# Attention with four heads a tile and exp columns as matmul weights, in a fused attention and feed-forward kernel

## The chip, the core and the metric

One core of a Trainium2 chip runs the whole program. The metric is device microseconds (us) of one execution, median of several runs. The kernel before took 488.79 us (three runs, 488.09 to 491.07). Runs more than 1.5% above the fastest of the same kernel count as slow and are not in the ratios.

Engines: TensorE (PE; its weight loads are PEld), VectorE (DVE), ScalarE (ACT), GpSimd (POOL) and SyncE (SP, which here only issues transfers).

## The reference

```python
# q, k, v: (8 batches, 12 heads, 448, 64) float32; tau = 0.1
q_n = q / (norm(q) + 1e-6);  k_n = k / (norm(k) + 1e-6)
scores = q_n @ k_n.T / tau
attn = softmax(scores);  x = (attn @ v)          # heads side by side: (3584, 768)
h = x @ w_in                                     # 768 -> 2048
g = h * sigmoid(1.702 * h)
out = g @ w_out                                  # 2048 -> 768
```

The kernel computes in float16 with float32 sums.

## The kernel before

It is written as a list of operations with durations, dependences and buffers. A small planner simulates them and emits each engine's instructions in the resulting order; engines then run in that order, as the changed kernel's trace shows: the last copy into the first scores' qkT ended at 16.26 us, but TensorE stood 0.50 us before the next transposes in its list, did them from 16.34 us, and began the scores at 17.09 us. So a duration in the list changes the order only.

Attention works on a pair of heads. The 448 positions lie as 4 chunks of 112 on partitions. Scores are keys by queries, so that exp gives the values product its operand without a transpose (code shortened):

```python
def scores(x, c):                       # one chunk of 112 keys, both heads: two matmuls on 64 rows
    for j in range(2):
        nc.tensor.matmul(out=sp[:, j, :S], lhsT=qkT[64*j:64*(j+1), 1, c*P:(c+1)*P],
                         rhs=qkT[64*j:64*(j+1), 0, :], start=True, stop=True)

def attend(x, j):                       # batches 2 to 7: v as weights, 448 exp columns streamed
    for c in range(C):
        nc.tensor.matmul(out=ps, lhsT=vts[x % NV][:, c, j], rhs=exps[x, c][:, j], ...)

def attend_h(x, h):                     # batches 0 and 1: 112 exp columns as weights, 65 of v streamed
    for i in range(2):
        for j in range(2):
            for c in range(C):
                at = (c % 2) * SH + i * P
                nc.tensor.matmul(out=ps[:P, o:o+D+1], lhsT=exps[x, h, c // 2][:, j, at:at+P],
                                 rhs=vts[x % NV][:, c, j, 63*j:63*j+D+1], ...)
```

`attend` gives the output transposed, with the softmax denominators in a row. To divide, the kernel sends the denominators through DRAM and back, spread over partitions (six transfers for three pairs). From batch 1 on, q and k are turned (transposed) by DMA; in batch 0 by TensorE. PSUM is shared out in buffers of 512 float32 columns: four for scores, three for the expert products and `attend_h` ("mm"), one for `attend`.

## Time and profile before

| | busy us of 485.7 | share |
|---|---|---|
| TensorE | 452.7 | 93% |
| ACT | 304.8 | 63% |
| DVE | 278.3 | 57% |
| POOL | 147.2 | 30% |
| DMA engines, 120 to 420 us | | 50% |

Read such a table with the stretches of time beside it: of TensorE's 33 us of idle time 23 lie in the first 80 us, and 5.4 between 120 and 420 us, where its own work is what counts.

### The profile page before, as it was taken

The page shows a single profiled execution, that of the slowest core. Times are in us where ns is not written, and L with a number is a line of the kernel's source. Part 1 is how long each engine was busy: PE and PEld are TensorE (multiplying, and loading weights), DVE is VectorE, ACT ScalarE, POOL GpSimd, SP SyncE. Part 2 cuts the span into 40 slices and gives each one's busy share as a digit, 9 for nine tenths or more (in the row PEclk, how much of TensorE's full clock was granted, in tenths as well). Part 3 has the DMA queues.
Part 4 walks back from the last instruction along what each step waited for, and adds up shares of the span by engine and source line. Part 5 has one row for each costly group of instructions (what it writes and reads, how often), then busy time and mean ns, then how long its engine had stood idle before and what let it go on. Part 6 is the DMA issues. An engine that isn't in the chain of part 4 may idle for free.

```text
span 485.7 us, 8249 instructions
## 1 busy us (share of the span) xinstructions
PE 452.7 (93%) x3008; PEld 253.5 (52%) x3008; DVE 278.3 (57%) x657; ACT 304.8 (63%) x479; POOL 147.2 (30%) x201
## 2 busy tenths in 40 slices
PE   0599995999998999999989999999999999999996
PEld 0477885864443554445434554445444554455563
DVE  7834784687689845866397645874264315532500
ACT  4755672899977676775776676774576546523411
POOL 1454675156751731406060421506000000000000
PEclk9999998999999999999999999999999999999999
DMA  9999299979977655647653556534320222022022
GB/s 207 230 236 252 44 198 146 270 195 268 248 205 166 154 151 167 138 97 193 143 140 101 144 140 170 133 94 122 86 47 3 61 67 61 2 62 66 0 57 75
DMA packets 87000, 64.83 MB, mean 133 GB/s; under 512 B 45800, under 2 KB 80432, under 8 KB 86960
## 3 DMA queue, kind: packets, MB, share of 16 engines
q1 hardware_dynamic: 83072, 57.79, 48.6%
q0 software_dynamic: 3648, 6.29, 7.1%
q8 instruction: 23, 0.38, 0.3%
q10 hardware_dynamic: 240, 0.23, 0.1%
q14 instruction: 17, 0.14, 0.1%
HBM read 49.81 MB, written 11.14 MB: 125 GB/s over the span
## 4 chain that ended last, share of the span: by engine, by line
PE 72%; DMA 12%; DVE 6%; SPq 4%; issue 2%; ACT 2%; POOL 2%; ACTq 0%; POOLq 0%; DVEq 0%
PE mm L546 28%; PE mm L491 18%; PE avp L356 8%; PE sp L337 6%; PE mm L402 4%; PE sp L385 3%; PE mm L521 3%; DMA qkT<-qks 3%; DMA k<-in_k_dram 2%; DMA q<-in_q_dram 2%; SPq L221 2%; DMA dnm<-den 2%; DMA v<-in_v_dram 2%; DVE xT L480 2%; POOL qks L291 1%
## 5 line engine op out<-in xcount | busy, mean ns | idle before, releaser
L348 ACT ACTIVATE expT<-sp 112x896 f16<-112x896 f32 x192 | 167.3, 918 | 60.1 <-PE sp L337 41.9
L546 PE MATMUL mm<-w_out,gT 128*128 128x384 f16 x896 | 154.6, 326 | 0.4 <-ACT ost L557 0.4
L491 PE MATMUL mm<-xT,w_in 128*128 128x448 f16 x672 | 134.6, 353 | 4.0 <-DVE gT L508 3.9
L546 PEld LDWEIGHTS <-gT 128*128 128x128 f16 x896 | 83.9, 98 | 65.6 <-issue 13.7
L491 PEld LDWEIGHTS <-w_in 128*128 128x128 f16 x672 | 63.1, 98 | 70.7 <-issue 16.0
L508 DVE SCALAR_TENSOR_TENSOR gT<-th,mm 128x448 f16<-128x448 f16 x112 | 67.7, 617 | 53.8 <-ACT th L501 53.5
L501 ACT ACTIVATE th<-mm 128x448 f16<-128x448 f32 x128 | 69.4, 546 | 44.2 <-PE mm L491 33.3
L240 DVE TENSOR_REDUCE n<-sq 112x8 f32<-112x512 f32 x96 | 63.7, 678 | 31.2 <-ACT sq L234 29.4
L303 POOL CAST vt<-v 112x256 f16<-112x256 f32 x84 | 33.9, 418 | 151.4 <-PE avp L356 116.9
L373 DVE TENSOR_SCALAR av<-avp 65x448 f16<-65x448 f32 x72 | 44.4, 616 | 48.9 <-PE avp L356 48.6
L356 PE MATMUL avp<-expT,vt 112*128 112x448 f16 x288 | 66.4, 352 | 1.4 <-DVE av L373 1.4
L291 POOL TENSOR_TENSOR qks<-k,y 112x512 f16<-112x512 f32 x48 | 50.8, 1058 | 49.7 <-DVE y L281 31.1
L557 ACT ACTIVATE ost<-mm 128x384 f32<-128x384 f32 x56 | 27.6, 492 | 45.3 <-PE mm L546 43.6
L291 POOL TENSOR_TENSOR qks<-q,y 112x512 f16<-112x512 f32 x47 | 49.8, 1061 | 0.0
L337 PE MATMUL sp<-qkT 64*112 64x448 f16 x288 | 43.0, 372 | 0.0
L480 DVE TENSOR_TENSOR xT<-av,rcb 64x448 f16<-64x448 f16 x72 | 36.7, 510 | 10.6 <-DMA rcb<-rcp 9.6
L356 PEld LDWEIGHTS <-vt 112*128 112x128 f16 x288 | 27.9, 97 | 26.4 <-issue 2.0
L234 ACT ACTIVATE sq<-k 112x512 f32<-112x512 f32 x42 | 26.5, 634 | 16.1 <-DMA k<-in_k_dram 14.6
L402 PE MATMUL mm<-vt,expT 112*112 112x65 f16 x384 | 30.9, 242 | 3.0 <-ACT expT L348 2.7
L402 PEld LDWEIGHTS <-expT 112*112 112x112 f16 x384 | 28.7, 161 | 6.3 <-ACT expT L348 3.7
L234 ACT ACTIVATE sq<-q 112x512 f32<-112x512 f32 x42 | 26.4, 633 | 7.7 <-DVE n L240 5.1
L385 PE MATMUL sp<-qkT 64*112 64x224 f16 x192 | 20.6, 325 | 8.1 <-DMA qkT<-qks 4.9
(39 smaller groups left out, 193.5 us busy)
## 6 DMA issues: line engine op xcount, KB each, us to landing
k<-in_k_dram SPq DMA_DIRECT2D x48, 224.0 KB, 3.7
v<-in_v_dram SPq DMA_DIRECT2D x48, 224.0 KB, 4.3
q<-in_q_dram SPq DMA_DIRECT2D x47, 224.0 KB, 4.3
rcb<-rcp SPq DMA_DIRECT2D x24, 168.0 KB, 3.5
w_in<-in_moe_w_in_dram POOLq DMA_DIRECT2D x2, 1536.0 KB, 16.8
w_out<-in_moe_w_out_dram POOLq DMA_DIRECT2D x2, 1536.0 KB, 14.6
out_dram<-ost SPq DMA_DIRECT2D x7, 336.0 KB
out_dram<-ost SPq DMA_DIRECT2D x8, 288.0 KB
```

The source lines that it names most:

```text
L234: return nc.scalar.activation(out=sqs[x, ti], in_=src, func=AF.Square)
L240: nc.vector.tensor_reduce(out=n2s[grp][:, x - grp[0], ti], in_=sqs.pop((x, ti)), axis=AX.X, op=ALU.add,)
L291: return eng.tensor_tensor(out=qkss[x][:, ti].rearrange("p c j d -> p j c d"), in0=src, in1=rss[x][:, ti, :, :, None].to_broadcast((P, 2, ...
L337: nc.tensor.matmul(out=sp[:, j, :S], lhsT=qkT[64 * j : 64 * (j + 1), 1, c * P : (c + 1) * P], rhs=qkT[64 * j : 64 * (j + 1), 0, :], start= ...
L348: nc.scalar.activation(out=e, in_=sps.pop(key)[:, :, :S], func=AF.Exp, scale=inv_tau, **kw)
L356: nc.tensor.matmul(out=ps, lhsT=vts[x % NV][:, c, j], rhs=exps[x, c][:, j], start=(c == 0), stop=(c == C - 1),)
L402: nc.tensor.matmul(out=ps[:P, o : o + D + 1], lhsT=exps[x, h, c // 2][:, j, at : at + P], rhs=vts[x % NV][:, c, j, 63 * j : 63 * j + D + 1 ...
L480: nc.vector.tensor_tensor(out=xT[r], in0=av[r, j], in1=rcbs[x // GRP][r, x % GRP], op=ALU.mult)
L491: nc.tensor.matmul(out=ps[:, :S], lhsT=w_in_sb[:, kk, 128 * m : 128 * (m + 1)], rhs=xTs[b, kk], start=(kk == 0), stop=(kk == KT1 - 1),)
L501: nc.scalar.activation(out=ths[key], in_=mms[key][:, :S], func=AF.Tanh, scale=0.851)
L508: nc.vector.scalar_tensor_tensor(out=gts[b // 2][:, m, (b % 2) * S : (b % 2 + 1) * S], in0=ths.pop((b, m)), scalar=1.0, in1=mms.pop((b, m) ...
L546: nc.tensor.matmul(out=mms[b2, t, n][:, :NW], lhsT=gts[b2][:, kk, 128 * t : 128 * (t + 1)], rhs=w_out_sb[:, kk, NW * n : NW * (n + 1)], st ...
```

## The change

The intent: the same mathematics with fewer and fuller instructions. q and k come four heads at a time on 128 partitions (7 column blocks of 64 positions), so keys fall in three chunks of 128 and a half chunk. The half chunks of two heads make one full-height product. The values product uses exp columns as weights in every batch, 128 of them, so the output has positions on partitions, the denominators lie beside it, and the round trip through DRAM goes.

```diff
-    C = S // P
+    C = S // 64
-    ps_s = psum("ps_s", 2);  ps_a = psum("ps_a", 1);  ps_m = psum("ps_m", 3)
+    ps_s = psum("ps_s", 2);  ps_m = psum("ps_m", 4)
 ...
+    def scores(y, *chunks):            # two chunks of 128 keys in a row
+        for g, n in chunks:
+            sp = sps[y, g, n] = ps_s.tile([128, 2, 512], FP32, name="sp")
+            score(sp, y, g, n, 0, S, 0)
+    def scores_l(y, h=None):           # half chunks of two heads: one product on 128 rows
+        for g in range(2):
+            nc.tensor.matmul(out=sp[:, g, :S], lhsT=kLs[y % NE][:, g], rhs=qkTs[y][:, g, 0], ...)
 ...
+    def attend(x, h, short=False):     # 14 matmuls: 2 of 130 columns, 12 of 65
+        for i in range(2):
+            a, m = P * (2 * h + i), P if short and i else 128
+            nc.tensor.matmul(out=o, lhsT=e[:, (C-1)*S + a : (C-1)*S + a + m], rhs=vt[:, 3] ...)
+            for n in range(3):
+                for j in range(2):
+                    at = (2 * n + j) * S + a
+                    nc.tensor.matmul(out=o[:, (D+1)*j : (D+1)*(j+1)], lhsT=e[:, at : at + m], rhs=vt[:, n, j], ...)
 ...
-    den_out, den_in, den_rcp, rcp_out, rcp_in, normalise   # the round trip through DRAM
+    dma_turn_x                                              # the output turned by DMA (batches 2 to 7)
+    TURNED = 2 * ND                     # batches 0 and 1: q, k and the output turned on TensorE
```

(Lines are joined and arguments left out. Cut: loads of v in four pieces, norms by Ln and Exp on ACT in batch 0, casts of v on POOL, w_in in eight pieces, new durations.)

## The prediction

> **What bounds the kernel now.** I read the page's busy table and slices first, then busy time by stretch, then the instructions in order of time, then the costliest groups, and the waits last.
>
> ```profile
> PE 452.7 (93%) x3008; PEld 253.5 (52%) x3008; DVE 278.3 (57%) x657; ACT 304.8 (63%) x479; POOL 147.2 (30%) x201
> ```
>
> TensorE is busy for 93% of the span. A share is an average, so the next view asks where the other 33 us are. Its columns are the stretch, its length, then busy time (and count) of PE, weight loads, DVE, ACT and POOL, then granted clock, DMA share and GB/s.
>
> ```profile
> 0.00:20.00 20.00, 5.18 (x42) 3.73 (x42) 15.34 (x60) 12.69 (x24) 6.59 (x12) 1.00 1.02 216
> 20.00:60.00 40.00, 37.02 (x349) 29.44 (x350) 21.33 (x61) 23.17 (x36) 20.96 (x23) 1.00 0.81 182
> 60.00:80.00 20.00, 14.83 (x193) 13.42 (x193) 13.68 (x44) 10.79 (x16) 12.69 (x16) 1.00 1.17 191
> 80.00:120.00 40.00, 39.61 (x394) 27.48 (x390) 28.45 (x78) 34.09 (x52) 20.22 (x32) 0.96 0.89 225
> 120.00:420.00 300.00, 294.61 (x1683) 144.74 (x1682) 182.15 (x387) 205.21 (x318) 86.71 (x120) 1.00 0.50 124
> ```
>
> From 80 us on TensorE practically never stops (294.6 of 300 us between 120 and 420), while ACT is at 68% and DVE at 61% there. The idle time sits in the first 20 us (14.8 us) and between 60 and 80 us (5.2 us). So whatever takes time off TensorE's stream from 80 us on shortens the kernel by the same amount; what ACT, DVE, POOL or DMA save there is not on the path. The stream itself, in order of time (start, length, instructions):
>
> ```profile
> 329.02 0.59 PE L337 MATMUL sp<-qkT 64*112 64x448 f16 x4
> 329.54 3.42 PE L546 MATMUL mm<-w_out,gT 128*128 128x384 f16 x20
> 332.80 0.92 PE L356 MATMUL avp<-expT,vt 112*128 112x448 f16 x4
> 333.65 0.58 PE L337 MATMUL sp<-qkT 64*112 64x448 f16 x4
> 334.17 3.42 PE L546 MATMUL mm<-w_out,gT 128*128 128x384 f16 x20
> ```
>
> Take starts, not lengths, because lengths overlap. Values product (4 matmuls): 333.65 - 332.80 = 0.85 us. Scores of two chunks (4 matmuls): 334.17 - 333.65 = 0.52 us. Twenty output matmuls: 332.80 - 329.54 = 3.26 us, 163 ns each. An attention turn costs 1.37 us, and a pair of heads needs two.
>
> The first batch's values product already has the form that the change wants everywhere (exp columns as weights, 65 columns streamed):
>
> ```profile
> 48.00 2.42 PE L521 MATMUL mm<-xT,w_in 128*128 128x224 f16 x12
> 50.22 0.39 PE L425 MATMUL mm<-ident,xs 112*128 112x112 f16 x2
> 50.40 2.34 PE L521 MATMUL mm<-xT,w_in 128*128 128x224 f16 x12
> 52.67 0.59 PE L385 MATMUL sp<-qkT 64*112 64x224 f16 x8
> 53.19 1.02 PE L402 MATMUL mm<-vt,expT 112*112 112x65 f16 x16
> 54.05 1.32 PE L521 MATMUL mm<-xT,w_in 128*128 128x224 f16 x12
> 55.30 0.40 PE L385 MATMUL sp<-qkT 64*112 64x224 f16 x4
> ```
>
> Two readings. Twelve matmuls of 224 columns take 50.22 - 48.00 = 2.22 us before 53 us and 55.30 - 54.05 = 1.25 us after: until about 53 us the array runs at half pace, although the clock column says 1.00. And 16 matmuls of 65 columns take 0.86 us at full pace, 54 ns each, twice what 65 columns need [...]: the 112-column weight load sets the pace, not the streaming. In that form the old attention saves nothing (two halves of 0.86 us against two heads of 0.85 us), which is why the old kernel used it in the first two batches only.
>
> ```profile
> L546 PEld LDWEIGHTS <-gT 128*128 128x128 f16 x896 | 83.9, 98 | 65.6 <-issue 13.7
> L402 PEld LDWEIGHTS <-expT 112*112 112x112 f16 x384 | 28.7, 161 | 6.3 <-ACT expT L348 3.7
> ```
>
> The load of 128 columns is recorded as 98 ns, that of 112 columns as 161 ns (part of it at half pace). The smaller load is the slower one.
>
> [...] Here scores (64 rows) between 128-row work: the turn's 0.85 + 0.52 us against 4 x 0.189 + 2 x 0.189 streamed (two 64-row matmuls run together) leaves 0.23 us for switching in and out.
>
> **The change part by part** ("duo" = four heads, two pairs).
>
> Scores. Before: four turns a duo of 0.52 + 0.09 us (the 0.09 is what 0.85 has over 4 x 0.19) = 2.44 us. After: 3 such turns, and the last half chunks of both heads as one full-height product, 2 x 0.19 = 0.38 us. 3 x 0.61 + 0.38 = 2.21 us.
>
> Values product. Before: 4 x 4 x 0.19 = 3.04 us a duo. After: four groups of 14 matmuls, 2 of 130 columns [...] and 12 of 65 ([...]I allow 34): 0.11 + 0.41 = 0.52 us, so 2.08 us. The diff's own plan writes 0.5. This 34 ns is an estimate that no part of this trace shows[...].
>
> Together 5.48 us a duo become 4.29, and 1.19 us x 18 duos (batches 2 to 7) = **21.4 us**, all on the bounding stream.
>
> First two batches. 24 groups of 16 become 24 of 14. At full pace 0.86 -> 0.52 us; at half pace a group was 1.63 us in the chain of waits and becomes about 2 x 0.11 + 12 x 0.06 = 0.94. About 15 x 0.34 + 9 x 0.69 = 11.3 us less TensorE work, less 42 new transposes for batch 1 at about 0.06 us = 2.5 us. As part of it lies where TensorE waits anyway, I count **7 us**.
>
> Batch 1's q and k are turned on TensorE, no longer by DMA. The wait list has one stall of 4.90 us at 79.6 us on that transfer, which took 13.5 us beside the expert weights, followed by 3.4 us at half clock (90.5 to 93.9). I count **5 us**, as batch 1's loads still queue behind w_in.
>
> Start. Tiles carry four heads, so the first k and q are 448 KB, not 224 KB: 2.1 us each at 216 GB/s, not 1.1; square, reduction and scaling run over 896 elements, not 512 (634 -> about 950 ns, 678 -> 1150, 1058 -> 1850); and in the order of instructions k of the second duo is scaled (behind v's casts) and turned ahead of the first scores. First scores came at 12.1 us; I expect about 18. **+5 us**.
>
> Off the path. ACT: 24 fewer exps of 918 ns a kernel, half as many squares, v's casts moved off. A batch from 2 on costs ACT about 21 x 0.92 + 6 x 0.95 + 16 x 0.55 + 7 x 0.49 = 37 us, DVE about 6 x 1.15 + 4.5 + 12 x (0.42 + 0.18) + 16 x 0.62 = 28 us, against TensorE's 16 x 1.14 + 112 x 0.163 + 3 x 4.29 = 49 us. The round trip of denominators through DRAM goes; it is worth nothing in the steady part. DMA turns become 36 of q and k halves and 36 of the output: 32,256 + 16,128 packets of 256 bytes against 37,632 now (24.8 ns of one engine each), and SyncE's issue grows.
>
> Sum: 488.8 - 21.4 - 7 - 5 + 5 = 460.4, say **460 us**.
>
> **Rivals.** (1) Weight loads stay the limit: if 65-column matmuls still pace at 54 ns, the four groups cost 3.05 us, a duo saves 0.2 us, and the time is about 483. For it: 54 ns is what this trace has for that form. Against: 98 ns against 161 in the loads, and the padding to 128 columns. (2) The start grows more than it saves: TensorE works through its instructions in order, so a late second k holds the first scores; 8 us more than counted, about 468. For: TensorE is idle 14.8 us there already and loads run at full DMA share. Against: the half-pace stretch from 20 to 60 us is 93% busy with work that shrinks. (3) DMA turns or PSUM buffers become a new wait: the output now reaches the products through transposes from SyncE, each 1.25 us to issue today, and the values product shares four buffers with the expert products. Perhaps +10 us, about 470. Against: DMA share is 0.50 and the plan keeps a batch's distance. (4) ACT becomes the bound: 37 against 49 us a batch, unlikely.
>
> **Range and chances.** With (2) or (3) mild the time is 465 to 475; with 30 ns matmuls and a free start about 450. Range **450 to 475**. Only (1), or (2) and (3) together, miss the 2% (479 us): faster 0.93, same 0.06, slower 0.01.
>
> **What would show it.** Steps between starts in the order of time: a group of 14 at about 0.52 us (0.75 would be rival 1), last chunks at 0.38 us, three score turns a duo; 128-column loads of exp near 98 ns; no stall on the transfer into qkT before the first full-width scores; first scores near 18 us. TensorE above 95% busy from 90 us to the end, with the last 61 us (224 output and 96 input products after the last attention) unchanged. Idle TensorE time from 120 us on over 6 us, put down to xT or to a PSUM release, would make it wrong.

The 0.52 us of a group (0.11 us for two matmuls of 130 columns, 34 ns for each of 65), its 0.94 us at half pace and the 30 ns in the range are estimates; no group of that form with 128 weight columns stands in the trace of the kernel before. The columns' own share can be estimated from two of its steps at full pace: twelve matmuls of 224 columns take 60.88 - 59.73 = 1.15 us, 96 ns each, and 96 of 448 columns take 460.53 - 442.37 = 18.16 us, 189 ns each. On the straight line through the two a column takes 0.42 ns (27 ns for 65), and whole steps are about 30 ns for 65 columns and 57 for 130. That matmuls of 65 columns keep to it behind loads of 128 was not shown then.

## The result

The changed kernel took 452.81 us (four runs, 452.04 to 453.23) against 489.71 us (four runs). The ratio is 0.9254 (95% interval 0.9216 to 0.9292). Ratios here are the mean time of one kernel's fast runs over that of the other's of the same rounds, so not quite the ratio of the medians. A later control of six runs of the same changed kernel gave 450.86 us (447.68 to 453.22) and 0.9202; so differences of 3 us between variants need care. All outputs are right.

The predicted range of 450 to 475 us held, and the forecast 460 was 7 us too high.

The page's busy line of the changed kernel, and busy time by stretch (same columns as before):

```profile
PE 414.7 (92%) x3614; PEld 249.9 (55%) x3614; DVE 233.1 (52%) x605; ACT 275.0 (61%) x417; POOL 149.7 (33%) x271
```

```profile
0.00:20.00 20.00, 4.72 (x35) 2.85 (x35) 16.36 (x57) 10.70 (x22) 8.76 (x20) 1.00 0.75 222
20.00:60.00 40.00, 35.26 (x411) 28.34 (x408) 23.81 (x65) 24.06 (x39) 23.33 (x34) 0.96 0.83 189
60.00:80.00 20.00, 18.57 (x248) 15.15 (x246) 17.49 (x55) 15.33 (x22) 12.21 (x19) 1.00 0.96 200
...
120.00:200.00 80.00, 73.52 (x682) 42.42 (x680) 47.53 (x119) 58.09 (x85) 35.31 (x67) 1.00 0.80 180
...
300.00:388.00 88.00, 88.00 (x760) 50.80 (x758) 32.48 (x82) 51.17 (x78) 12.61 (x25) 1.00 0.29 63
```

TensorE lost 38.0 us of busy time and still bounds the kernel. The idle 5.2 us between 60 and 80 us shrank to 1.4. In its place stand 6.5 us between 120 and 200 us, where the old kernel had 1.9 (from the sums below): a new wait. Batches 2 to 7 in order of time:

```profile
248.28 0.55 PE L381 MATMUL sp<-qkT 64*128 64x448 f16 x4
248.76 2.12 PE L568 MATMUL mm<-w_out,gT 128*128 128x384 f16 x12
250.72 0.22 PE L444 MATMUL mm<-vt,exp 128*128 128x130 f16 x1
250.78 0.35 PE L455 MATMUL mm<-vt,exp 128*128 128x65 f16 x6
250.97 0.22 PE L444 MATMUL mm<-vt,exp 128*128 128x130 f16 x1
251.03 0.35 PE L455 MATMUL mm<-vt,exp 128*128 128x65 f16 x6
251.22 0.54 PE L407 MATMUL sp<-qkT,kL 128*128 128x448 f16 x2
251.60 2.11 PE L568 MATMUL mm<-w_out,gT 128*128 128x384 f16 x12
```

A group of 14 takes 251.22 - 250.72 = 0.50 us. Six matmuls of 65 columns take 250.97 - 250.78 = 0.19 us, 32 ns each. Scores of two chunks take 248.76 - 248.28 = 0.48 us, the half chunks 251.60 - 251.22 = 0.38 us.

In the first batch the array is at full pace much earlier:

```profile
40.13 2.47 PE L543 MATMUL mm<-xT,w_in 128*128 128x224 f16 x24
42.44 0.22 PE L444 MATMUL mm<-vt,exp 128*128 128x130 f16 x1
```

Twenty-four matmuls of 224 columns take 42.44 - 40.13 = 2.31 us, 96 ns each, where the old kernel still needed 185 ns at 48 us. The trace's record of the granted clock begins with full pace at 33.5 us here and at 52.5 us before. For the time ahead of it there is no record (the page's clock row shows full pace), and that it was half pace is read from the steps: seven transposes take 104 ns each at 22.2 us and 57 ns each at 66.3 us.

To see where every microsecond went, I summed over TensorE's instructions the time from one start to the next (or to the instruction's own end, if the engine was then idle). These sums add up to the span:

| us | before | changed | difference |
|---|---|---|---|
| values product | 89.5 | 56.4 | -33.1 |
| scores | 56.6 | 48.6 | -8.0 |
| turns of q and k | 5.6 | 8.2 | +2.5 |
| turns of the output | 4.3 | 4.5 | +0.1 |
| first expert product (all batches) | 149.7 | 149.8 | +0.1 |
| second expert product | 147.0 | 147.2 | +0.2 |
| idle | 33.0 | 36.8 | +3.8 |
| span | 485.7 | 451.5 | -34.3 |

### The profile page after: what moved, and what is told of

Same layout as the page of the kernel before. It is cut to its first block, busy times and chain, and to the rows that moved or that the text cites.

```text
span 451.5 us, 9300 instructions
## 1 busy us (share of the span) xinstructions
PE 414.7 (92%) x3614; PEld 249.9 (55%) x3614; DVE 233.1 (52%) x605; ACT 275.0 (61%) x417; POOL 149.7 (33%) x271
## 4 chain that ended last, share of the span: by engine, by line
PE 66%; DMA 10%; POOL 6%; SPq 6%; issue 5%; DVE 4%; ACT 3%; POOLq 0%; ACTq 0%; DVEq 0%
PE mm L568 29%; PE mm L513 24%; PE mm L455 5%; PE sp L381 5%; DMA qk<-in_k_dram 4%; SPq L230 4%; DMA v<-in_v_dram 3%; POOL qks L316 3%; PE mm L444 2%; ACT exp L416 2%; PE sp L407 1%; DMA out_dram<-ost 1%; DMA qkT<-qks 1%; POOL sq L242 1%; SPq L217 1%
## 5 line engine op out<-in xcount | busy, mean ns | idle before, releaser
L416 ACT ACTIVATE exp<-sp 128x896 f16<-128x896 f32 (+1 forms) x171 | 148.2, 905 | 38.0 <-PE sp L381 32.8
L523 ACT ACTIVATE th<-mm 128x448 f16<-128x448 f32 x128 | 69.5, 548 | 51.4 <-PE mm L513 41.0
L316 POOL TENSOR_TENSOR qks<-qk,y 128x512 f16<-128x512 f32 (+2 forms) x63 | 73.0, 1188 | 11.5 <-issue 5.3
L249 DVE TENSOR_REDUCE n<-sq 128x14 f32<-128x896 f32 x48 | 51.4, 1078 | 36.5 <-ACT sq L243 36.4
L455 PE MATMUL mm<-vt,exp 128*128 128x65 f16 (+1 forms) x1152 | 60.8, 197 | 1.8 <-ACT exp L416 1.8
L455 PEld LDWEIGHTS <-exp 128*128 128x128 f16 (+1 forms) x1152 | 54.1, 101 | 13.0 <-issue 5.4
L327 POOL CAST vt<-v 128x384 f16<-128x384 f32 x48 | 24.3, 506 | 109.2 <-PE mm L455 41.1
L243 ACT ACTIVATE sq<-qk 128x896 f32<-128x896 f32 x42 | 39.6, 950 | 28.3 <-DMA qk<-in_k_dram 21.7
L467 DVE RECIPROCAL rc<-mm 112x4 f32<-112x4 f32 x96 | 17.1, 178 | 68.7 <-PE mm L455 68.6
L444 PE MATMUL mm<-vt,exp 128*128 128x130 f16 x192 | 43.3, 225 | 5.3 <-DVE gT L530 4.7
L381 PE MATMUL sp<-qkT 64*128 64x448 f16 (+1 forms) x324 | 43.1, 348 | 1.9 <-ACT exp L416 1.6
L475 DVE TENSOR_TENSOR xs<-mm,rc 112x256 f16<-112x256 f32 x72 | 30.5, 424 | 2.5
## 6 DMA issues: line engine op xcount, KB each, us to landing
w_out<-in_moe_w_out_dram POOLq DMA_DIRECT2D x2, 1536.0 KB, 15.1
```

Of the source, the lines that this page charges most:

```text
L243: return nc.scalar.activation(out=sqs[y, ti], in_=src, func=AF.Square)
L249: nc.vector.tensor_reduce(out=n2s[grp][:, y - grp[0], ti], in_=sqs.pop((y, ti)), axis=AX.X, op=ALU.add,)
L316: insts.append(eng.tensor_tensor(out=qkss[y][:, ti, first : first + step * (n - 1) + 1 : step].rearrange("p c j d -> p j c d"), in0=src[:, ...
L381: nc.tensor.matmul(out=sp[:, j, at : at + qn], lhsT=qkT[r, g, 1, 128 * n : 128 * (n + 1)], rhs=qkT[r, g, 0, q0 : q0 + qn], start=True, sto ...
L416: return nc.scalar.activation(out=dst, in_=src, func=AF.Exp, scale=inv_tau, **ekw)
L444: nc.tensor.matmul(out=o, lhsT=e[:, (C - 1) * S + a : (C - 1) * S + a + m], rhs=vt[:, 3].rearrange("p j d -> p (j d)"), start=True, stop=F ...
```

## The experiments

Twelve kernels ran. Nine start from the changed kernel (a_...), one of them is the control, and three are steps from the kernel before (b_...). They ran on several chips, so variants are compared by their ratios to the kernel before, which ran beside each. The sums of TensorE's steps named below are made as in the table above.

### a_m112: 112 weight columns instead of 128

```diff
-            a, m = P * (2 * h + i), P if short and i else 128
+            a, m = P * (2 * h + i), P
```

> The changed kernel, with 112 instead of 128 exp columns loaded as weights in every values product; results are the same. Theory (the fast load of 128 columns is what makes the values product cheap): a group of 14 goes from 0.50 to about 14 x 54 ns = 0.76 us, 96 groups x 0.26 = 25 us, so about 477 us; and the half-pace stretch at the start, which ended near 33 us, lasts longer again[...]. Rival (streaming 65 columns in place of 448 with half the loads hidden is what pays, the width of the load is nothing): a group stays at 0.50 us, 453 us.

Measured: 468.01 us (462.07 to 468.47), ratio 0.9531. In order of time, at full pace:

```profile
245.45 0.22 PE L444 MATMUL mm<-vt,exp 128*112 128x130 f16 x1
245.51 0.45 PE L455 MATMUL mm<-vt,exp 128*112 128x65 f16 x6
245.80 0.24 PE L444 MATMUL mm<-vt,exp 128*112 128x130 f16 x1
...
246.16 1.30 PE L513 MATMUL mm<-xT,w_in 128*128 128x448 f16 x6
```

Six matmuls of 65 columns now take 245.80 - 245.51 = 0.29 us, 48 ns each in place of 32, and a group 0.71 us. The groups of weight loads (operand, count, busy us, mean ns) of this run and of the changed kernel:

```profile
L455 PEld LDWEIGHTS <-exp 128*112 128x112 f16 x1152 | 79.3, 141 | 5.5 <-issue 1.9 <-ACT exp L416 0.6
```

```profile
L455 PEld LDWEIGHTS <-exp 128*128 128x128 f16 (+1 forms) x1152 | 54.1, 101 | 13.0 <-issue 5.4 <-ACT exp L416 2.4
```

The narrower load takes 141 ns, the wider one 101. (The edit also makes the output 112 rows high; that the load is what counts rests on these two figures.) So the theory holds: the values product grew by 23.5 us (79.9 against 56.4). But the time grew by only 15 us, not the 25 expected, as idle time fell by 9.7 us (27.1 against 36.8). That a slower TensorE waits less for the other engines would explain it; no run tests that.

The changed kernel holds the same comparison within itself: in batch 0 one block in four is loaded with 112 columns. In order of time, at full pace:

```profile
37.45 0.45 PE L455 MATMUL mm<-vt,exp 128*112 128x65 f16 x6
37.74 0.22 PE L444 MATMUL mm<-vt,exp 128*128 128x130 f16 x1
37.80 0.35 PE L455 MATMUL mm<-vt,exp 128*128 128x65 f16 x6
37.99 0.24 PE L444 MATMUL mm<-vt,exp 128*112 128x130 f16 x1
```

Six matmuls take 37.74 - 37.45 = 0.29 us behind loads of 112 columns and 37.99 - 37.80 = 0.19 us behind loads of 128.

The second reading came true in this pair: half pace, which ended at 33.5 us in the changed kernel, ended at 48.3 us here. It is not shown that the width alone decides it: the other profiles with 128 columns (without a_warm's edit) first came to full pace between 25.1 and 35.0 us, but b_half128m4 only at 46.8 us.

### b_half: the old half-width form in all batches

```diff
-    HALF = 2 * HP
+    HALF = NPAIR
 ...                                   # and turned_h of a pair's second half after its first
```

> The kernel before, with its own form for batches 0 and 1 used in all batches: exp columns as weights, 112 of them, output turned on TensorE, no round trip of denominators. Theory (this form alone does not pay): a group of 16 stays at 0.86 us against 0.85 us for one head in the old form, and per pair the turns of the output (4 x 0.06 us) and the switches of half-width scores come on top, 0.2 to 0.5 us x 36 pairs: 496 to 508 us. Rival (what pays is the form, or the round trip and the DMA turns that it removes): 480 us or less.

Measured: 498.51 us (498.13 to 498.74), ratio 1.0189 (1.0142 to 1.0236: clear of 1). The theory holds: exp columns as weights, with the round trip through DRAM gone, make the kernel 9 us slower as long as 112 columns are loaded. The values product's sum is 93.4 us against 89.5, and turns of the output add 8.2 us. In order of time (to compare with the next run):

```profile
242.93 0.98 PE L402 MATMUL mm<-vt,expT 112*112 112x65 f16 x16
243.84 0.59 PE L385 MATMUL sp<-qkT 64*112 64x224 f16 x8
```

### b_half128: the same with 128 weight columns

```diff
+    ebufs, eturn = [const.tile([P, 2, S + 16], FP16, name=f"eb{i}") for i in range(8)], [0]
...
-                        out=ps[:P, o : o + D + 1],
-                        lhsT=exps[x, h, c // 2][:, j, at : at + P],
+                        out=ps[:, o : o + D + 1],
+                        lhsT=exps[x, h, c // 2][:, j, at : at + 128],
```

> As b_half, and 128 exp columns loaded as weights instead of 112 (exp tiles padded by 16 columns; the 16 extra output rows are not read). Theory: a group of 16 goes from 0.86 to 16 x 32 ns = 0.51 us, 96 x 0.35 = 33 us less than b_half, so 465 to 475 us, and the half-pace stretch at the start ends earlier than 53 us: most of the whole change from a padding of 16 columns. Rival (the gain needs q and k on 128 partitions and 3.5 chunks): within 5 us of b_half.

Measured: 481.52 us (478.10 to 481.92), ratio 0.9828 (0.9777 to 0.9878: clear of 1): 6.5 us above the range of the theory, and 17 us from b_half where the rival had 5. In order of time:

```profile
242.48 0.65 PE L404 MATMUL mm<-vt,eb 112*128 112x65 f16 x16
243.07 0.59 PE L387 MATMUL sp<-qkT 64*112 64x224 f16 x8
243.59 1.31 PE L493 MATMUL mm<-xT,w_in 128*128 128x448 f16 x6
246.13 0.27 PE L427 MATMUL mm<-ident,xs 112*128 112x112 f16 x2 [1.23 <-DVE xs L417]
```

A group of 16 takes 243.07 - 242.48 = 0.59 us with the switch into scores, which in b_half took 243.84 - 242.93 = 0.91 us. The sum fell by 34.2 us (59.2 against 93.4), as expected. Idle time rose by 15.6 us (45.1 against 29.5). The last line shows such a wait: TensorE stands 1.23 us before the turn of the output, for DVE's division. The half pace at the start ended earlier only in part: full pace came at 35.0 us (51.4 in b_half), but half pace returned from 38.4 to 48.6 us.

### b_half128m4: a fourth shared PSUM buffer

```diff
-    ps_a = psum("ps_a", 1)
-    ps_m = psum("ps_m", 3)
+    ps_m = psum("ps_m", 4)
 ...                                   # batch 0's transposes of q and k take "mm" instead of "a"
```

> b_half128 with the first batch's transposes in the shared buffers, so that PSUM has four of them for products and values, as in the changed kernel, not three and one that only the first batch uses. b_half128 gained 34 us of TensorE's steps over b_half but gave back 16 us as idle time (45.1 us against 29.5). Theory (three shared buffers caused that): idle falls to about 35 us and the time to 470 to 474 us. Rival (the waits come from the order of ACT and DVE, or from the output's turns on TensorE waiting for DVE): idle stays above 42 us, 478 to 483 us.

Measured: 470.86 us (470.20 to 475.35), ratio 0.9659. Idle time 37.4 us, close to the 35 expected. Three shared buffers had held back part of what the padding gained; of the 16 us given back as idle time, 7.6 returned. Between 120 and 400 us idle time was 2.3 us in b_half and 11.4 in b_half128, and is 3.5 here. (The planner's order changes with the buffer; the two are tested together.) The largest wait left is one on the transfer into qkT at 77 us, 8.3 us long, the stall that the changed kernel does not have.

So the padding with the fourth buffer gives about half of the whole change (ratio 0.9659 against 0.9254). By the sums the changed kernel is 17.7 us shorter still than this one: 8.5 us in scores, 7.3 in turns of the output and 4.2 in the values product, less 2.6 more in turns of q and k, and 1 us in small terms. That half comes with four heads a tile, full-width scores and the output turned by DMA; a_turn1 and a_singles test parts of it.

### a_turn1: batch 1 turned by DMA again

```diff
-    TURNED = 2 * ND
+    TURNED = ND
```

> The changed kernel, with batch 1's q and k (and its output) turned by DMA as in the kernel before, not on TensorE. My prediction counted 5 us for this part less 2.5 us for the transposes. Theory: the stall on the transfer into qkT comes back, 5 us or more between 55 and 80 us, and the time is 456 to 462 us. Rival (something else holds batch 1 anyway, such as its loads behind w_in or POOL's scaling): 451 to 454 us.

Measured: 467.50 us (466.35 to 468.04), ratio 0.9553: the right direction, but some 15 us where 3 to 9 were expected. The granted clock (the last column but two) shows part of it. Busy time by stretch of this run:

```profile
60.00:80.00 20.00, 15.67 (x112) 10.76 (x111) 8.92 (x29) 4.71 (x8) 12.20 (x23) 0.91 1.16 198
80.00:100.00 20.00, 17.40 (x193) 10.23 (x192) 10.89 (x30) 17.62 (x24) 7.26 (x16) 1.00 1.03 246
100.00:120.00 20.00, 12.64 (x113) 6.77 (x112) 13.59 (x39) 15.36 (x20) 9.73 (x17) 0.59 1.09 219
```

Idle time is 46.2 us against 36.8. From 103.6 to 124.1 us the clock was granted at half pace, after a row of waits for exp. By the sums idle time is 9.4 us more and the products' steps are 8.4 us longer, less 4.9 us of turns that this run does by DMA. All four runs show the lower mean clock (0.960 to 0.963; the changed kernel's show 0.987 to 0.996). The stall on qkT itself did not come back; TensorE ran the second expert product instead and waited for w_out (4.3 us), and batch 1's attention moved to 80 to 120 us, where ACT had to give its exps in haste. Turning batch 1 on TensorE (its output too) is thus worth about 15 us here, through the order it allows and the clock that came with it, and not the 5 us of one stall. That the waits caused the half pace is not tested.

### a_singles: scores one chunk at a time

```diff
-            for t, chunks in enumerate((((0, 0), (0, 1)), ((0, 2), (1, 0)), ((1, 1), (1, 2)))):
+            for t, chunks in enumerate((((0, 0),), ((0, 1),), ((0, 2),), ((1, 0),), ((1, 1),), ((1, 2),))):
-                    takes=[("sp", 2), ...
+                    takes=[("sp", 1), ...
```

> The changed kernel, with scores planned one chunk at a time (each taking one PSUM buffer) instead of in twos. Theory (twos save switches of the tiling): each chunk that stands alone pays the switch of about 0.2 us again; if half of the 126 chunks of batches 1 to 7 stand alone, about +6 us, 456 to 464 us. Rival (the planner puts two in a row anyway, as it did in the kernel before, where they stood in fours): 451 to 455 us.

Measured: 463.79 us (461.18 to 464.11), ratio 0.9469: the theory holds. In the trace 109 of the 126 chunks of full width stand alone. One alone, in order of time:

```profile
244.57 1.30 PE L513 MATMUL mm<-xT,w_in 128*128 128x448 f16 x6
245.80 0.36 PE L381 MATMUL sp<-qkT 64*128 64x448 f16 x2
246.09 2.44 PE L513 MATMUL mm<-xT,w_in 128*128 128x448 f16 x12
```

It takes 0.29 us, two in a row 0.48. The way in costs another 0.10 us each time (245.80 - 244.57 = 1.23 us for six matmuls of 0.19). So two alone cost 0.78 us, two in a row 0.58, and 109 / 2 times 0.2 us make 11 us, close to the measured 11 to 13 us over the changed kernel and its control. But the kernel before already had its scores in fours of matmuls in 69 of 75 places, so twos are no gain of the change; they had to be kept.

### a_exp2: ACT's saving taken away

```diff
         if h is None:
+            exp_of(dst, sp[:, :, :S])
             return exp_of(dst, sp[:, :, :S])
```

> The changed kernel, with the exp of the last half chunks done twice in batches 1 to 7 (same values): 21 x 0.92 = 19 us more ACT work, nearly all that the 3.5 chunks saved. Theory (ACT's saving is off the path, as predicted): under 3 us, 452 to 456 us. Rival (the chunks pay through ACT: TensorE waits for exp or for PSUM that ACT holds): at least half of it comes through, 462 us or more.

Measured: 451.18 us (448.05 to 454.84), ratio 0.9201 (0.9144 to 0.9258). Against the control's 0.9202 no part of 19 us more ACT work shows; the intervals leave room for some 3 us, not for the rival's half. ACT's saving was off the path.

### a_warm: TensorE kept busy before its first work

```diff
+        for _ in range({(0, 1): 245, (0, 0): 70}.get((y, ti), 0)):
+            nc.tensor.matmul(out=ps32[:, 448:512], lhsT=ident, rhs=ident[:, :64], start=True, stop=True)
```

> The changed kernel, with 245 unused matmuls of 64 columns on TensorE before the first transposes and 70 before the second, in the time in which it is idle, into columns of the same buffer that nobody reads. Theory (the half pace of TensorE up to 33 us is on the path): TensorE runs at full pace from about 5 us on, first transposes 0.4 us instead of 0.8, products of experts begin 3 us earlier than at 40.1 us, 448 to 451 us. Rival (the start is set by loads, ACT and POOL[...]): 452 to 454 us.

Measured: 448.57 us (445.25 to 450.96), ratio 0.9164, in two clusters (445 to 446 and 451). This was the first sign that one kernel spreads by 5 us. The clock was granted in full at 5.4 us, but cut again from 19.1 to 25.9 us and from 29.3 to 32.8 us, and expert products began at 39.5 us, not some 3 us before the changed kernel's 40.1 (the control's began at 39.6). With the control's 0.9202 beside it, no gain can be claimed.

### a_again, a_dma4, a_dma4w, a_early: the new wait

One wait of the changed kernel, in order of time on all engines (numbers in brackets: idle time before, and what ended it):

```profile
282.80 1.31 PE L513 MATMUL mm<-xT,w_in 128*128 128x448 f16 x6
...
283.76 0.95 ACT L243 ACTIVATE sq<-qk 128x896 f32<-128x896 f32 x1 [3.57 <-DMA qk<-in_q_dram]
284.62 0.53 ACT L523 ACTIVATE th<-mm 128x448 f16<-128x448 f32 x1
...
285.75 0.61 DVE L530 SCALAR_TENSOR_TENSOR gT<-th,mm 128x448 f16<-128x448 f16 x1
...
286.41 0.27 PE L444 MATMUL mm<-vt,exp 128*128 128x130 f16 x1 [2.30 <-DVE gT L530]
...
287.99 0.58 PE L513 MATMUL mm<-xT,w_in 128*128 128x448 f16 x1
```

ACT stands 3.57 us before a square, for a load of q that was issued at 277.5 us. Behind the square stand the tanh, the gate, and with it a shared PSUM buffer, so the values product waits 2.30 us. The planner had placed the square where it expected the load to have landed: it counts 1.9 us a transfer plus its packets, while the profile's list of transfers has 4.5 us for k and 5.7 us for q from issue to landing. Two waits between 120 and 200 us stand behind such squares too:

```profile
182.71 0.95 ACT L243 ACTIVATE sq<-qk 128x896 f32<-128x896 f32 x1 [2.44 <-DMA qk<-in_k_dram]
...
184.51 0.54 PE L407 MATMUL sp<-qkT,kL 128*128 128x448 f16 x2 [2.11 <-ACT exp L416]
...
194.97 0.95 ACT L243 ACTIVATE sq<-qk 128x896 f32<-128x896 f32 x1 [2.57 <-DMA qk<-in_k_dram]
...
197.87 0.99 PE L568 MATMUL mm<-w_out,gT 128*128 128x384 f16 x5 [1.39 <-DVE gT L530]
```

They are 3.5 of the 6.5 us of idle time there, and 1.2 us more at 131 and 133 us follow another late square (2.30 us at 129.5 us). The largest of the rest, 1.64 us at 122 us, is a wait of the values product for a gate that stands behind norms in DVE's order.

Three kernels and a control went on one chip:

```diff
-DMA_US = 1.9
+DMA_US = 4.0                                                            # a_dma4; a_dma4w: with a_warm's edit
-        early = due_of(grp[0]) - (5 if first else 8)
+        early = due_of(grp[0]) - (5 if first else 7)                    # a_early alone
```

> The changed kernel unaltered, as the control of the runs beside it: 452 to 454 us, idle TensorE time of 6 us between 120 and 200 us as in its first profile. If it shows two clusters of times some 5 us apart, as three variants of it did, differences under 5 us between variants are not explained from single runs.

> The changed kernel, with the planner's fixed time of a transfer set from 1.9 to 4.0 us, nearer to what the profile shows from issue to landing (4.5 and 5.7 us for k and q); only the order of instructions changes. Theory (the idle TensorE time after 120 us comes from squares that stand in ACT's order before their k or q has landed, which holds tanh, gate and so a PSUM buffer): idle after 120 us falls from about 9 us to under 4, time 446 to 450 us. Rival (the four shared PSUM buffers hold it whatever the order): idle stays, 451 to 455 us.

> a_dma4 with the unused matmuls of a_warm at the start. If both help and do not overlap, 3 to 4 us less than a_dma4: 442 to 447 us. If the warm start only shifts the waits, the same as a_dma4.

> The changed kernel, with squares and norms planned one unit (a quarter of a duo's turn) later from batch 1 on. Theory of late landings: a little less idle TensorE time than in the changed kernel, 449 to 453 us. Rival: the norms then come late for the scaling and the DMA turns, and the time is 454 us or more.

| | median us | range | ratio (95%) | idle TensorE 120 to 400 us, in its profile |
|---|---|---|---|---|
| a_again (control) | 450.86 | 447.68 to 453.22 | 0.9202 (0.9165 to 0.9239) | 5.7 |
| a_dma4 | 444.43 | 442.71 to 447.36 | 0.9086 (0.9050 to 0.9122) | 4.1 |
| a_dma4w | 445.82 | 444.11 to 446.66, and 450.95 (slow) | 0.9102 (0.9075 to 0.9129) | 2.1 |
| a_early | 445.28 | 443.16 to 446.07 | 0.9090 (0.9059 to 0.9121) | 5.5 |

The control missed its forecast: five of its six runs lie below 452 us. Its profiled run (447.68 us) has no wait at 284 us and no half pace from 32.1 us to its end; the first profile (453.23 us) had both, at half pace from 54.0 to 57.4 us and from 286.1 to 289.5 us. By these two profiles, part of the spread is whether such waits and cuts of the clock happen in a run.

Both changes of order gave 5 to 6 us, more than the interval of either, and both came in below the ranges forecast for them. They beat both kernels: a_dma4 has 0.9086 of the kernel before. The cause is only partly shown. The wait of the kind above is absent from a_dma4 between 200 and 400 us (idle 0.0 us there, control 0.3, first profile 2.7), but the control's profile had almost lost it as well, and a_early's has one such wait of 2.66 us and is as fast. For the theory speak the two waits shown at 184 and 197 us: the control has them too (2.12 and 1.51 us), and both changed orders have lost them (a_dma4 has one of 1.29 us at 169 us in their place). From 120 us on ACT stands before a square for its load 11 times in the changed kernel (23.7 us), 12 times in the control (20.0 us), 5 times in a_dma4 (5.6 us) and 8 times in a_early (14.6 us). What remains is that late landings do stand in ACT's order, that planning for them is faster, and that one profile each does not divide the 5 us among the waits. The warm start again added nothing: in a_dma4w unused matmuls fill TensorE's first 40 us, and the time is not better.

## Why the prediction was right, and where it was off

**The bound: right.** TensorE stayed the bound at 92% busy, and 19 us of ACT work added in a_exp2 did not show. From 90 us on it is idle for 15.1 of 361.5 us, so the 95% expected there held. After the last attention matmul the order of work is as expected: 224 output and 132 input matmuls in 61.4 us (before 224 and 126, not the 96 of the prediction, in 60.2 us). The prediction's own sign of being wrong, over 6 us of idle time from 120 us on put down to xT or to PSUM, was nearly met: idle time up to 400 us is 9.2 us (5.4 before), and three waits of the values product for a gate, which holds a PSUM buffer, are 4.7 us of it.

**The values product at 34 ns: right, 32 measured.** That a load of 128 columns would let it through was the estimate, from loads of 98 and 161 ns; a_m112 shows it by changing the width alone: loads of 141 ns in place of 101, 48 ns a step and 468 us. b_half and b_half128 show it from the other side: the form alone loses 9 us, and 128 columns take 17 us off that, to 8 us below the kernel before. Rival 1 feared 54 ns and about 483 us; even without the wide load (a_m112) it is 48 ns and 468 us.

**The steady saving of 1.19 us a duo: slightly small.** 0.50 us for a group instead of 0.52, and 0.48 us for scores instead of 0.52, make 3 x 0.58 + 0.38 + 4 x 0.50 = 4.12 us instead of 4.29. That is 1.36 us x 18 = 24.5 us in place of 21.4. The score loads of 128 columns are recorded with 97 ns, those of 112 with 123 ns, so the shorter score turn fits the same cause; no run separates it.

**The first two batches, 7 us: the mis-sized term.** The sums up to 120 us, where both kernels have done nearly the same batches, fell by 11.8 us for the values product (predicted 11.3), but I took a discount for time in which TensorE waits anyway. Scores fell by 2.9 us as well, and batch 0's expert products by 1.4 us (21.6 to 20.1 us over all of them), which fits full pace at 33.5 us and not at 52.5. Less 2.5 us for the new transposes this is 13.6 us, twice what I counted. That half pace would end earlier was not in my sum. a_m112 (48.3 us) points to the width of the weights, b_half128m4 (46.8 us with 128 columns) to something beside it; that stays open.

**Batch 1's stall, 5 us: right in sign, wrong as a step.** The stall went (idle before the transfer into qkT: 4.9 us before, none after), but a_turn1 shows that the part is worth some 15 us. I had priced one wait, where the choice decides the order of everything from 60 to 140 us. I also misplaced the half clock that followed: it lay at 79.8 to 83.2 us, not 90.5 to 93.9.

**The start, +5 us: right in the event, wrong in the cost.** First scores came at 17.1 us (expected about 18, before 12.1), held from 16.26 us on by the second k's turns, as expected. But TensorE's idle time up to 40 us is the same in both kernels (17.6 and 17.7 us), and by then the changed one had done 8 groups of its values product against 5. The later start cost nothing that the trace shows.

**Rivals 2 and 3.** The new wait of rival 3 exists, though not through the output's transposes: between 120 and 200 us idle time grew by 4.6 us, about what the removed stall had given. Of the 6.5 us there, 4.7 stand behind squares that wait for their loads in ACT's order, as the section on the new wait shows. b_half128m4 shows the weight of the shared PSUM buffers: with a fourth, the median falls by 10.7 us (8 us by the ratios).

Together: -24.5 (steady part, by its steps) - 13.6 (first batches) + 3.8 (idle time, predicted 0) = -34.3 us of span, against -28.4 in the prediction. The table's sums divide it a little differently: 26.4 us off the steady attention, and 1.8 us more in the other products. The prediction landed high because the first two batches saved 6.6 us more than was counted and the steady part 3.1 us more. The start's 5 us, which were not paid, stood in its sum against the stall's 5 us, and new waits (3.8 us more idle time) took part of the gain back; so some of the closeness to 460 is errors that cancel.

## What to carry to other kernels

Look at the weight side of a stream of small matmuls. Here 65-column matmuls stepped at 48 ns behind loads of 112 columns (a_m112) and at 32 ns behind loads of 128 (the changed kernel), where their columns alone need about 27 ns by the estimate under the prediction. So a load of fewer than 128 columns may be the pace, and padding it to 128 can pay even though more is loaded: it took 17 us off b_half. Other widths were not run. A faster stream can then need one more PSUM buffer (b_half128m4: 37.4 us of idle time in place of 45.1), or it gives part of its gain back as waits. Price the removal of a stall by what order it allows and not by the one wait that the profile shows, and give the planner landing times that the profile has measured (here 4.5 and 5.7 us in place of 1.9).

## What the traces show of TensorE beside this

- Loads and steps: the loads of exp are recorded with 141 ns at 112 columns (a_m112) and 101 ns at 128 (the changed kernel), and the step of 65-column matmuls is 48 against 32 ns. So the recorded length of a load is not the pace: the kernel before has 54 ns a step at full pace, with loads of 161 ns (part of them at half pace).
- Transposes: seven of 128 columns took 0.40 us (66.25 to 66.65 us of the changed kernel), 57 ns each.
- Full pace at the start: in the kernel before TensorE was recorded as busy 37.0 of 40 us from 20 to 60 us and still came to full pace only at 52.5 us; with 112 columns loaded it did so at 48.3 us (a_m112) and 51.4 us (b_half), with 128 between 25.1 and 35.0 us in eight profiles and at 46.8 us in one (b_half128m4). What decides it is not shown.
- Cuts of the clock: in the changed kernel half pace of 3.4 us began once at 54.0 us, 0.9 us after a wait of 1.1 us, and once at 286.1 us, within a wait of 2.3 us.
- Scores on 64 rows between work on 128: in the changed kernel six matmuls of 65 columns take 0.29 us before them (247.99 to 248.28 us) and 0.19 us elsewhere, so the way in costs 0.10 us; two chunks take 0.48 us (248.28 to 248.76 us) where two steps of 448 columns make 0.38, so the way out costs another 0.10 us by this estimate. In a_singles 109 chunks alone cost some 11 us by the count above.
